# Later weight splits and scatters, scans two groups ahead and fixed input rings in a fused attention, expert and max-out kernel

## Chip, cores and metric

The kernel runs on one core of a Trainium2 chip. The metric is the device time of one execution in microseconds (us), the median of several runs. Rows of the trace come from one profiled execution.

## What is computed

Three layers in a row, all in float32 at the ends:

```python
for t in range(S):                      # B,H,S,D = 4,8,768,48
    state = alpha[t][:, None] * state + k[t] (x) v[t]
    y[t] = q[t] @ state                 # linear attention with decay
x = y as 3072 rows of 384
expert = argmax(xn @ en.T); gate = softmax(...)[expert]
x = gate * (relu(x @ w1[expert]) @ w2[expert])      # 8 experts, F = 1024
h = max(x @ w1, x @ w2, x @ w3); out = h @ w_out    # 384 -> 768 -> 384
```

## The kernel before

**Stage 1: groups.** The attention is done in 24 groups of 128 tokens (`NT`), all eight heads of a batch entry at once, six groups per batch entry. The code's loop `for g in range(NT)` writes out the order of instructions on every engine by hand (`manual_schedule`): each engine runs its own queue in exactly that order and waits on semaphores. For one group:

- `load(i)` brings the inputs of two groups (`at` decays, `kt`, `qt`, `vt`) through SP's queue, from tile pools with 3 or 4 buffers; a buffer is written again only when its last reader is done.
- `undo`, `invert`, `decay` (L270 to L293): two scans on VectorE (DVE), a reciprocal, then a product on GpSimd (POOL) that scales `qt`. They stand three groups ahead of the group that is finished.
- `spread` (L295): two copies on ScalarE (ACT) that put the scaled `qt` into the block tile `bdq`, two groups ahead.
- `keys`: a DVE product that scales `kt`.
- `scores` (TensorE, PE, L315), `causal` (DVE, L323), `sv` (PE, L350), `qs` (PE, L358, then the ACT copy `xt`, L361). In the first group of a batch entry `qs` has no products.
- `ranges` (ACT, L308): an absolute sum for a check at the end.
- `by_token` (PE, L368, then two ACT instructions), `kback` (PE transposes and an ACT copy), `logits` (DVE), `update` (PE, L389, then DVE products into `sbar`).

**Routing and scatters.** After 4 (later 2) groups a generator `route(i)` takes the argmax of their logits and counts places for the tokens: five DVE steps, then counting products on PE (`rk`, L418 to L421), then four DVE steps. `slot("P")`, `slot("A")` and so on step it on at marked places of the loop, by a string with a letter for each step. Its last step makes four (two) token groups `ready`, and `scatter` (L480, an indirect DMA issued by POOL) writes a group's 128 rows to `xs` in memory. The first scatter waits for the eight `zero_rows` DMAs (L238). When 18 groups have been scattered, `fetch_first` reads back the first 224 rows of expert 0 (`xa`).

**Weights.** `load_w` brings raw expert weights at the groups in `LOADS`. `split_w` cuts them into a high and a low part: two ACT casts (L222, L223) at the end of a group in `SPLITS`, and in the next group, after `slot("P")`, a POOL and a DVE subtraction (L225, L226).

**The end of stage 1.** `turn_first` transposes `xa`, the last `route` is run with the product `up` of the first weights beside it, the last scatters go out, and `fetch(0)` reads expert 0's further rows (`xb`), which waits for every scatter. **Stage 2** (from about 183 us) is the experts and the max-out layer, an almost gapless stream of PE products.

Of the kernel before, what the change touches and what calls it, by code (L numbers as in the profile page):

```python
# [35 lines left out]
CAP = max(CAPS)  # L36
AW = 224
AG = 18
NA = 5
LOADS = (8, 11, 16, 20)  # L40
SPLITS = (12, 14, 16, 18, 20)
ROW = DM + 2
TB = 512
BLOCKS = (256,) + (TB,) * 5 + (256,)
# [14 lines left out]
def fused_kernel(ctx, tc, qT, kT, aT, vn, emb, tau, w1, w2, m1, m2, m3, mo,  # L59
# [27 lines left out]
    loads = {}  # L87
    W = NP * C
    WE = NP * CE

    def load(i):

        b, c2 = divmod(i, NCH // 2)
        w = 2 * W
        o = c2 * w
        we = 2 * WE
        at = ld.tile([HR, we + 1], F32, tag="at", name=f"at_{i}", bufs=3)
        kt = ld.tile([HR, w], F32, tag="kt", name=f"kt_{i}")
        qt = ld.tile([HR, w], F32, tag="qt", name=f"qt_{i}")
        vt = ld.tile([128, 2, NP, HR], F32, tag="vt", name=f"vt_{i}")  # L100
        loads[i] = (at, kt, qt, vt)
        if i > 0:
            nc.sync.dma_start(at, aT[b, :, c2 * we:(c2 + 1) * we + 1])
            for t, src in ((kt, kT), (qt, qT)):
                nc.sync.dma_start(t, src[b, :, o:o + w])
            nc.sync.dma_start(vt, vn[b, :, 2 * c2:2 * c2 + 2])
            return
        for n in range(2):
            sl = slice(n * W, (n + 1) * W)
            if n == 0:  # L110
                nc.sync.dma_start(at[:, 0:WE + 1], aT[b, :, 0:WE + 1])
            nc.sync.dma_start(kt[:, sl], kT[b, :, sl])
            nc.sync.dma_start(qt[:, sl], qT[b, :, sl])
            if n == 0:
                nc.sync.dma_start(at[:, WE + 1:], aT[b, :, WE + 1:2 * WE + 1])
            nc.sync.dma_start(vt[:, n], vn[b, :, n])
# [70 lines left out]
        nc.gpsimd.iota(tokid[:, :, 1], pattern=[[1, NT]], base=0, channel_multiplier=NT)  # L187

    def constants_rest():
        nc.vector.tensor_sub(tri, mask, ident)  # L190
        nc.vector.tensor_copy(dec, dec_i)
        nc.vector.tensor_copy(base_b[0:1, :], base_i[0:1, :])

    def warm(ps, n):
        for _ in range(n):
# [74 lines left out]
    def undo(g):  # L270

        at, kt, qt, vt = loads[g // 2]
        o, oe = (g % 2) * W, (g % 2) * WE
        cur[g] = dict(bd=bdq[g % 3], qh=qt[:, o:o + W], kh=kt[:, o:o + W], v=vt[:, g % 2],
                      at=at[:, oe:oe + WE])
        cur[g]["PR"] = PR = wk.tile([HR, 2, WE], F32, tag="PR", name=f"PR_{g}", bufs=4)
        R = PR[:, 1]
        nc.vector.tensor_tensor_scan(R[:, ::-1], at[:, oe + 1:oe + WE + 1][:, ::-1], last[:, ::-1], 0.0, ALU.mult, ALU.add)
        cur[g]["R"] = R

    def by_pair(x, n=CE):
        return x.rearrange("p (a t) -> p a t", t=n)

    def invert(g):
        nc.vector.reciprocal(by_pair(first[g % 2])[:, :, 0], by_pair(cur[g]["R"])[:, :, 0])

    def decay(g):

        t = cur[g]
        P = t["PR"][:, 0]  # L290
        nc.vector.tensor_tensor_scan(P, t["at"], first[g % 2], 0.0, ALU.mult, ALU.add)  # L291
        qh = by_pair(t["qh"], C)
        nc.gpsimd.tensor_mul(qh, qh, by_pair(P)[:, :, 0:C])  # L293

    def spread(g):  # L295
        t = cur[g]
        for j in range(2):
            r = slice(j * 64, j * 64 + D)
            nc.scalar.copy(t["bd"][r, :, j], by_pair(t["qh"][r], C))
# [53 lines left out]
    def qs(g):  # L353
        t = cur[g]
        if g % NCH > 0:
            for p in range(NP):
                for j in range(2):
                    nc.tensor.matmul(t["xT"][own(j), p], t["sbar"][own(j), p], t["qh"][own(j), p * C:(p + 1) * C],  # L358
                                     start=False, stop=(p == NP - 1), skip_group_check=True)
        t["xs"] = wk.tile([HR, NP, C], F32, tag="xt", name=f"xt_{g}")  # L360
        nc.scalar.copy(t["xs"], t["xT"])  # L361
# [16 lines left out]
    def tokens(g):  # L378
        cur[g]["xr"] = xr = wk.tile([128, ROW], F32, tag="xr", name=f"xr_{g}", bufs=13)
        nc.gpsimd.tensor_copy(xr[:, DM:ROW].bitcast(I32), tokid[:, g])  # L380
# [95 lines left out]
    def step(it):  # L476
        return next(it, None)

    def scatter(pos, xr):
        r = nc.gpsimd.indirect_dma_start(out=xs, out_offset=bass.IndirectOffsetOnAxis(ap=pos, axis=0),  # L480
                                         in_=xr, in_offset=None, bounds_check=E * N - 1, oob_is_err=False).ins
        tc.declare_no_dep(r, group="scatters", reason="no two tokens take the same row")
        if 0 in exp:
            tc.declare_no_dep(r, group="first", reason="later tokens take other rows, or the general path runs")
        for z in zeroed:
            tc.add_manual_dep(r, z.name, DATA)
        tc.add_to_no_dep_group("scatters", r)
        placed.append(r)
# [122 lines left out]
    def slot(x):  # L611
        for c in chains:
            while c[1] and c[1][0] == x:
                step(c[0])
                c[1] = c[1][1:]

    with tc.manual_schedule():
        wm = ps_s.tile([128, 512], F32, tag="sr", name="wm")
        warm(wm, NWARM)
        emb_steps = embedding()  # L620
        step(emb_steps)
        for f in (undo, invert, decay, keys):
            f(0)
            step(emb_steps)
        spread(0)
        turn_base()
        undo(1)
        step(emb_steps)
        invert(1)
        step(emb_steps)  # L630
        decay(1)
        scores(0, 0)
        keys(1)
        scores(0, 1)
        for _ in emb_steps:
            pass
        embedding_turn()
        spread(1)
        causal(0, 0)
        causal(0, 1)  # L640
        wx = ps_x.tile([128, 512], F32, tag="xp", name="wx")
        warm(wx, NWARMX)
        load(2)
        constants_pool()
        kback(0)
        undo(2)
        invert(2)
        decay(2)
        ranges(0)
        constants_rest()  # L650
        zt = clear_scratch()

        ends = [sum(SIZES[:i + 1]) for i in range(len(SIZES))]
        splits = iter(())
        for g in range(NT):
            if g % 2 == 0 and 3 <= g // 2 + 3 < NT // 2:
                load(g // 2 + 3)
            if g < E:
                zero_rows(zt, g)
            if g in ends:  # L660
                i = ends.index(g)
                chains.append([route(i), "EEABCPABCE" if SIZES[i] > 2 else "EEEEEPABCE"])
            tokens(g)
            sv(g, 0)
            sv(g, 1)
            slot("P")
            step(splits)
            if g + 3 < NT:
                undo(g + 3)
            slot("A")  # L670
            for _ in range(1 if g < AG else 2):
                if g >= 8 and ready:
                    scatter(*ready.pop(0))
            if g > 0:
                by_token(g - 1)
            if g + 1 < NT:
                kback(g + 1)
            if g + 3 < NT:
                invert(g + 3)
            if g + 2 < NT:  # L680
                spread(g + 2)
            if g + 3 < NT:
                decay(g + 3)
            slot("B")
            if g + 1 < NT:
                for hf in range(2):
                    scores(g + 1, hf)
                    causal(g + 1, hf)
            slot("C")
            qs(g)  # L690
            if g + 1 < NT:
                ranges(g + 1)
            if g < NT - 2:
                keys(g + 2)
            if g > 0:
                logits(g - 1)
            update(g)
            slot("E")
            for _ in range(1 if g < AG else 2):
                if g >= 8 and ready:  # L700
                    scatter(*ready.pop(0))
            if len(placed) >= AG and 0 not in exp:
                fetch_first()
            if g in LOADS:
                load_w(LOADS.index(g))
            if g in SPLITS:
                splits = split_w(SPLITS.index(g))
                step(splits)
        turn_first()
        by_token(NT - 1)  # L710
        logits(NT - 1)
        chain = route(len(SIZES) - 1)
        for _ in range(5):
            step(chain)
        a = up(*order[0])
        for _ in chain:
            pass
        for r in ready:
            scatter(*r)
        a()  # L720
        keep(exp[0]["xa"], meta[0:AW], "ids_a")
        for n in (1, 2):
            up(*order[n])()
    pctx.close()
    ectx = ExitStack()
    pools["y"] = ectx.enter_context(tc.tile_pool(name="ps_y", bufs=1, space=PSUM))
# [426 lines left out]
```

## Time and profile before

| | us |
|---|---|
| median of 3 runs (709.54 to 712.46) | 711.03 |
| the profiled execution, its own time | 717.39 |
| span of its instructions | 715.7 |
| PE / DVE / ACT / POOL busy | 684.0 / 420.4 / 290.2 / 292.3 |

The span runs from the first to the last instruction; some 1.7 us of the execution's time lie around it. Busy shares are means over both stages. DVE is busy for 17 of the first 20 us and for less than a fifth of the last 100, so the means say nothing of stage 1. A matmul's end is modelled, so PE can look a little busier than it is.

### The profile page before, as it was taken

The numbers are of one execution on the slowest core, as the hardware profiler recorded it, in microseconds if no ns is written. First come the engines' busy times: TensorE is split into PE (matmuls) and PEld (weight loads), VectorE is DVE, ScalarE is ACT, GpSimd is POOL, SyncE is SP. The second block draws the span as 40 slices with busy tenths as digits, with TensorE's granted clock in tenths as the row PEclk, the third lists the DMA queues.
The fourth block names the chain that finished last, engine by engine and source line by source line (L and its number), as shares of the span: only waits on it lengthen the run. The fifth ranks groups of instructions, "written<-read, shape, count | busy, mean of one in ns | idle before, by whom it ended". The sixth has DMA issues, their size and how long they took to land. (4 is left out here: it accounts for less than half of the span.)

```text
span 715.7 us, 11937 instructions
## 1 busy us (share of the span) xinstructions
PE 684.0 (96%) x4467; PEld 610.0 (85%) x4467; DVE 420.4 (59%) x772; ACT 290.2 (41%) x617; POOL 292.3 (41%) x310
## 2 busy tenths in 40 slices
PE   7999799888999999999999999999999999999994
PEld 4788677668988999999999998888888898898994
DVE  8899698875478888888998699211311311303110
ACT  4676576654345445554545322321211212212221
POOL 5331746443134454554555366432333224233331
PEclk9999899999999999999999999999999999999998
DMA  9999965031355447546454220000000000000000
GB/s 231 265 274 247 255 185 187 23 108 69 109 153 174 136 147 212 173 157 204 139 178 149 46 67 24 24 15 30 1 22 23 1 22 23 0 23 23 12 34 26
DMA packets 30817, 75.01 MB, mean 105 GB/s; under 512 B 8600, under 2 KB 10400, under 8 KB 30752
## 3 DMA queue, kind: packets, MB, share of 16 engines
q1 hardware_dynamic: 26880, 64.68, 32.1%
q0 software_dynamic: 3840, 9.48, 3.7%
q8 instruction: 37, 0.61, 0.4%
q14 instruction: 28, 0.23, 0.1%
q10 hardware_dynamic: 32, 0.01, 0.0%
HBM read 62.26 MB, written 11.90 MB: 104 GB/s over the span
## 5 line engine op out<-in xcount | busy, mean ns | idle before, releaser
L931 DVE TENSOR_TENSOR t<-p,t 128x512 f32<-128x512 f32 (+1 forms) x84 | 51.6, 614 | 189.8 <-PE p L927 187.1
L925 PE MATMUL p<-bxh,m 128*128 128x512 f32 (+1 forms) x378 | 137.0, 362 | 0.0
L927 PE MATMUL p<-bxl,m 128*128 128x512 f32 (+1 forms) x378 | 137.0, 362 | 0.0
L926 PE MATMUL p<-bxh,m 128*128 128x512 f32 (+1 forms) x378 | 137.0, 362 | 0.0
L225 POOL TENSOR_TENSOR w<-r,w 128x384 fp32r<-128x384 f32 x64 | 71.4, 1117 | 80.8 <-ACT w L222 80.8
L938 POOL TENSOR_TENSOR fl<-t,fh 128x512 fp32r<-128x512 f32 (+1 forms) x36 | 43.5, 1208 | 139.3 <-ACT fh L937 104.2
L937 ACT CAST fh<-t 128x512 fp32r<-128x512 f32 (+1 forms) x42 | 23.5, 559 | 149.3 <-DVE t L931 149.3
L927 PEld LDWEIGHTS p<-bxl,m 128*128 128x128 f32 x378 | 71.1, 188 | 12.3
L925 PEld LDWEIGHTS p<-bxh,m 128*128 128x128 f32 x378 | 71.1, 188 | 11.9
L926 PEld LDWEIGHTS p<-bxh,m 128*128 128x128 f32 x378 | 71.1, 188 | 11.9
L572 PE MATMUL h<-xh,w 128*128 128x224 f32 (+8 forms) x207 | 72.2, 349 | 0.0
L573 PE MATMUL h<-xh,w 128*128 128x224 f32 (+8 forms) x207 | 70.4, 340 | 0.3 <-POOL w L225 0.3
L574 PE MATMUL h<-xl,w 128*128 128x224 f32 (+8 forms) x207 | 70.1, 339 | 0.0
L226 DVE TENSOR_TENSOR w<-r,w 128x384 fp32r<-128x384 f32 x64 | 60.4, 944 | 16.3 <-ACT w L223 16.3
L602 PE MATMUL y<-hl,w 128*128 128x464 f32 (+8 forms) x192 | 66.3, 345 | 0.0
L600 PE MATMUL y<-hh,w 128*128 128x464 f32 (+8 forms) x192 | 65.8, 343 | 0.0
L601 PE MATMUL y<-hh,w 128*128 128x464 f32 (+8 forms) x192 | 65.8, 343 | 0.0
L582 ACT ACTIVATE hh<-h 128x464 fp32r<-128x464 f32 (+8 forms) x64 | 32.0, 501 | 61.6 <-PE h L574 61.6
L315 PE MATMUL sc<-bdq,kt 112*128 112x256 f32 x192 | 51.1, 414 | 1.7 <-POOL bdq L175 1.7
L293 POOL TENSOR_TENSOR qt<-qt,PR 112x512 f32<-112x512 f32 x24 | 29.2, 1217 | 51.8 <-DVE PR L291 21.0
L583 DVE SCALAR_TENSOR_TENSOR hl<-h,hh 128x464 fp32r<-128x464 f32 (+8 forms) x64 | 36.2, 566 | 22.5 <-ACT hh L582 22.4
L946 PE MATMUL o<-wo,fh 128*128 128x384 f32 x144 | 48.4, 336 | 0.0
(206 smaller groups left out, 1415.4 us busy)
## 6 DMA issues: line engine op xcount, KB each, us to landing
r<-in_w SPq DMA_DIRECT2D x64, 384.0 KB, 3.7
cr_in_m<-in_m SPq DMA_DIRECT2D x18, 384.0 KB, 5.0
at<-in_aT SPq DMA_DIRECT2D x11, 451.9 KB, 11.4
kt<-in_kT SPq DMA_DIRECT2D x11, 448.0 KB, 11.6
qt<-in_qT SPq DMA_DIRECT2D x11, 448.0 KB, 10.0
vt<-in_vn SPq DMA_DIRECT2D x11, 448.0 KB, 11.1
exr<-xs_scratch SPq DMA_DIRECT2D x5, 675.5 KB, 6.1
xs_scratch<-zt SPq DMA_DIRECT2D x8, 289.5 KB, 12.6
```

The costliest lines, as they stand in the source:

```text
L225: nc.gpsimd.tensor_sub(a[:, 1], r1[:, k], a[:, 0].bitcast(F32))
L226: nc.vector.tensor_sub(b[:, 1], r2[:, k], b[:, 0].bitcast(F32))
L572: nc.tensor.matmul(hp, a[:, 0, k], t["xh"][:, k, c], start=(k == 0), stop=False)
L573: nc.tensor.matmul(hp, a[:, 1, k], t["xh"][:, k, c], start=False, stop=False)
L574: nc.tensor.matmul(hp, a[:, 0, k], t["xl"][:, k, c], start=False, stop=(k == KD - 1))
L600: nc.tensor.matmul(y, w[:, 0, sl], hh, start=(f == 0 and c.start == 0), stop=False, skip_group_check=True)
L601: nc.tensor.matmul(y, w[:, 1, sl], hh, start=False, stop=False, skip_group_check=True)
L602: nc.tensor.matmul(y, w[:, 0, sl], hl, start=False, stop=(f == NF1 - 1), skip_group_check=True)
L925: nc.tensor.matmul(pt, m[:, 0, k], xh[:, k], start=(k == 0), stop=False)
L926: nc.tensor.matmul(pt, m[:, 1, k], xh[:, k], start=False, stop=False)
L927: nc.tensor.matmul(pt, m[:, 0, k], xl[:, k], start=False, stop=(k == KD - 1))
L931: nc.vector.tensor_tensor(t0, pt, t0, op=ALU.max)
```

## The change

Seven things, all in stage 1:

1. `LOADS` go from (8, 11, 16, 20) to (14, 16, 21, 23), `SPLITS` from (12, 14, 16, 18, 20) to (19, 20, 21, 22, 23); the last split ends after the loop.
2. Scatters begin at group 9, not 8, and are at most two per group to the end (before: four per group from group 18). The first of a group's two stands behind the POOL product of `decay`, no longer ahead of it; `tokens` stands behind it too.
3. For pairs of groups the counting products move from the top of a group (`P`) to a new slot `Q` ahead of `qs` in the same group, and the four last steps follow in that group's `E`.
4. `undo`, `invert` and `decay` stand two groups ahead; `spread` stands one group ahead, at the top of the loop. The prologue loses one `undo`, `invert`, `decay` and `spread`.
5. `at`, `kt`, `qt` live in rings of four fixed tiles. From the fifth load on, each is read by two DMAs of 48 rows that leave out the 16 rows between two heads (before: one DMA of 112 rows). `at` gets one more buffer, `PR` one fewer.
6. Three small constants move from DVE to POOL and ACT; group 0's `qt` product moves from POOL to DVE.
7. After the loop two `up` products are issued before the last counting, not one.

```diff
-LOADS = (8, 11, 16, 20)
-SPLITS = (12, 14, 16, 18, 20)
+SC0 = 9
+LOADS = (14, 16, 21, 23)
+SPLITS = (19, 20, 21, 22, 23)
+NRING = 4
...
+    rings = {n: [ld.tile([HR, w], F32, tag=f"{n}{s}", name=f"{n}{s}", bufs=1) for s in range(NRING)]
+             for n, w in (("at", 2 * WE + 1), ("kt", 2 * W), ("qt", 2 * W))}
...
+            for r in (slice(0, HR),) if i < NRING else (slice(0, D), slice(64, HR)):
+                nc.sync.dma_start(at[r], aT[b, r, c2 * we:(c2 + 1) * we + 1])
+                for t, src in ((kt, kT), (qt, qT)):
+                    nc.sync.dma_start(t[r], src[b, r, o:o + w])
...
-        nc.vector.tensor_sub(tri, mask, ident)
-        nc.vector.tensor_copy(dec, dec_i)
-        nc.vector.tensor_copy(base_b[0:1, :], base_i[0:1, :])
+        nc.gpsimd.tensor_sub(tri, mask, ident)
+        nc.scalar.copy(dec, dec_i)
+        nc.scalar.copy(base_b[0:1, :], base_i[0:1, :])
...
-                chains.append([route(i), "EEABCPABCE" if SIZES[i] > 2 else "EEEEEPABCE"])
-            tokens(g)
+                chains.append([route(i), "EEABCPABCE" if SIZES[i] > 2 else "EEEEEQEEEE"])
+            if g + 1 < NT:
+                spread(g + 1)
             sv(g, 0)
             sv(g, 1)
             slot("P")
             step(splits)
-            if g + 3 < NT:
-                undo(g + 3)
+            if g + 2 < NT:
+                undo(g + 2)
             slot("A")
-            for _ in range(1 if g < AG else 2):
-                if g >= 8 and ready:
-                    scatter(*ready.pop(0))
             if g > 0:
                 by_token(g - 1)
             if g + 1 < NT:
                 kback(g + 1)
-            if g + 3 < NT:
-                invert(g + 3)
             if g + 2 < NT:
-                spread(g + 2)
-            if g + 3 < NT:
-                decay(g + 3)
+                invert(g + 2)
+                decay(g + 2)
+            if g >= SC0 and ready:
+                scatter(*ready.pop(0))
+            tokens(g)
             slot("B")
...
             slot("C")
+            slot("Q")
             qs(g)
...
             slot("E")
-            for _ in range(1 if g < AG else 2):
-                if g >= 8 and ready:
-                    scatter(*ready.pop(0))
+            if g >= SC0 and ready:
+                scatter(*ready.pop(0))
...
-        a = up(*order[0])
+        a = [up(*order[n]) for n in range(2)]
...
-        a()
+        for f in a:
+            f()
+        step(splits)
```

## Rows read from the trace of the kernel before

**Rows 1.** Windows: stretch, us, busy (count) PE PEld DVE ACT POOL, clock, DMA, GB/s.
```profile
26.78:59.41 32.63, 32.45 (x382) 27.54 (x384) 31.01 (x61) 25.03 (x53) 8.25 (x12) 1.00 1.04 269
26.78:142.19 115.41, 105.42 (x1144) 88.14 (x1144) 100.46 (x197) 78.27 (x167) 46.84 (x53) 0.94 0.75 203
65.10:83.20 18.10, 14.26 (x142) 11.75 (x144) 12.11 (x28) 8.17 (x17) 8.89 (x9) 0.81 1.04 256
112.56:121.61 9.05, 7.38 (x68) 5.80 (x70) 8.20 (x13) 3.81 (x9) 7.18 (x7) 0.81 0.80 256
142.19:169.43 27.24, 23.08 (x265) 19.20 (x266) 18.16 (x50) 14.60 (x32) 10.78 (x13) 0.94 0.25 86
148.93:159.58 10.65, 7.83 (x76) 6.46 (x78) 6.76 (x18) 5.05 (x11) 3.46 (x5) 0.84 0.39 132
183.00:715.70 532.70, 522.79 (x2818) 477.56 (x2818) 271.08 (x448) 179.45 (x378) 217.18 (x205) 1.00 0.26 78
```

**Rows 2.** Timeline of one undisturbed group: start, us, engine, line, tiles, idle before.
```profile
43.46 0.59 ACT L361 COPY xt<-xT 112x512 f32<-112x512 f32 x1 [0.68 <-PE xT L358]
...
44.07 1.06 ACT L308 ACTIVATE jk<-PR 112x1032 bf16<-112x1032 f32 x1
...
45.04 0.19 ACT L308 ACTIVATION_READ_ACCUMULATOR jk<-PR 112x1 f32 x1
...
46.19 1.91 PE L315 MATMUL sc<-bdq,kt 112*128 112x256 f32 x8
...
47.26 1.25 ACT L299 COPY bdq<-qt 48x512 f32<-48x512 f32 x2
...
48.00 1.18 POOL L293 TENSOR_TENSOR qt<-qt,PR 112x512 f32<-112x512 f32 x1 [4.01 <-DVE sm L413]
...
48.02 1.08 PE L358 MATMUL xT<-qt,sbar 48*48 48x128 f32 x16
...
49.15 0.58 ACT L361 COPY xt<-xT 112x512 f32<-112x512 f32 x1 [0.63 <-PE xT L358]
```

**Rows 3.** Timeline of POOL: the first scatter.
```profile
71.89 1.26 POOL L480 DMA_INDIRECT xs_scratch<-xr,pos  x1 [11.93 <-DMA r<-in_w]
```

**Rows 4.** Instructions of tile zt: the zeroing DMAs, their issues and landings.
```profile
L238 SPq DMA_DIRECT2D xs_scratch<-zt x8: 577/580/730, 21.8 to 51.8; - x8
...
DMA to landing us min/median/max: 9.9/12.6/13.2
```

**Rows 5.** Instructions of line 480: the scatters, their durations (ns) and landings.
```profile
L480 POOL DMA_INDIRECT xs_scratch<-xr,pos x24: 966/1000/1749, 71.9 to 176.5; - x24
...
DMA to landing us min/median/max: 2.6/3.4/9.6
```

**Rows 6.** Timeline of group 10: a POOL product beside a DVE product.
```profile
88.38 1.20 POOL L293 TENSOR_TENSOR qt<-qt,PR 112x512 f32<-112x512 f32 x1
88.48 1.66 DVE L304 TENSOR_TENSOR kt<-kt,PR 112x512 f32<-112x512 f32 x1
```

**Rows 7.** Timeline: a weight split in group 13, counting products in group 21.
```profile
96.13 0.51 ACT L223 CAST w<-r 128x384 fp32r<-128x384 f32 x1
...
96.67 1.05 DVE L226 TENSOR_TENSOR w<-r,w 128x384 fp32r<-128x384 f32 x1 [1.04 <-ACT w L223]
...
153.57 0.17 PE L420 MATMUL rk<-oh,ones_b 128*128 128x8 bf16 x1 [2.82 <-DVE oh L415]
```

**Rows 8.** Timeline of DVE at the start: the last scan before group 1's mask.
```profile
17.12 1.87 DVE L291 TENSOR_TENSOR_SCAN PR<-at,first 112x516 f32<-112x516 f32 x1
...
18.92 0.66 DVE L323 TENSOR_TENSOR ss<-sc,mask 128x512 f32<-128x512 f32 x1
```

**Rows 9.** Timeline of the end: last places, last scatter.
```profile
174.16 0.17 DVE L431 CAST pos<-sm 128x2 uint32<-128x2 f32 x1
...
176.47 0.98 POOL L480 DMA_INDIRECT xs_scratch<-xr,pos  x1 [0.30 <-issue]
```

**Rows 10.** DMA issues from 140 to 184 us: KB each, us to landing.
```profile
xa<-xs_scratch SPq DMA_DIRECT2D x1, 337.8 KB, 3.2
```

More of the change, by code (lines that the diff above doesn't have):

```diff
@@ L96, in load @@
         we = 2 * WE
-        at = ld.tile([HR, we + 1], F32, tag="at", name=f"at_{i}", bufs=3)
-        kt = ld.tile([HR, w], F32, tag="kt", name=f"kt_{i}")
-        qt = ld.tile([HR, w], F32, tag="qt", name=f"qt_{i}")
+        at, kt, qt = (rings[n][i % NRING] for n in ("at", "kt", "qt"))
         vt = ld.tile([128, 2, NP, HR], F32, tag="vt", name=f"vt_{i}")
@@ L102, in load @@
         if i > 0:
-            nc.sync.dma_start(at, aT[b, :, c2 * we:(c2 + 1) * we + 1])
-            for t, src in ((kt, kT), (qt, qT)):
-                nc.sync.dma_start(t, src[b, :, o:o + w])
+            for r in (slice(0, HR),) if i < NRING else (slice(0, D), slice(64, HR)):
+                nc.sync.dma_start(at[r], aT[b, r, c2 * we:(c2 + 1) * we + 1])
+                for t, src in ((kt, kT), (qt, qT)):
+                    nc.sync.dma_start(t[r], src[b, r, o:o + w])
             nc.sync.dma_start(vt, vn[b, :, 2 * c2:2 * c2 + 2])
@@ L275, in undo @@
                       at=at[:, oe:oe + WE])
-        cur[g]["PR"] = PR = wk.tile([HR, 2, WE], F32, tag="PR", name=f"PR_{g}", bufs=4)
+        cur[g]["PR"] = PR = wk.tile([HR, 2, WE], F32, tag="PR", name=f"PR_{g}", bufs=3)
         R = PR[:, 1]
@@ L292, in decay @@
         qh = by_pair(t["qh"], C)
-        nc.gpsimd.tensor_mul(qh, qh, by_pair(P)[:, :, 0:C])
+        (nc.gpsimd if g else nc.vector).tensor_mul(qh, qh, by_pair(P)[:, :, 0:C])
     def spread(g):
@@ L637, in fused_kernel @@
         embedding_turn()
-        spread(1)
         causal(0, 0)
@@ L645, in fused_kernel @@
         kback(0)
-        undo(2)
-        invert(2)
-        decay(2)
         ranges(0)
@@ L719, in fused_kernel @@
             scatter(*r)
-        a()
+        for f in a:
+            f()
+        step(splits)
         keep(exp[0]["xa"], meta[0:AW], "ids_a")
-        for n in (1, 2):
-            up(*order[n])()
+        up(*order[2])()
     pctx.close()
```

## The prediction

> **What bounds the kernel now.** I read the windows first, with edges at the `xt` copies that end a group's products. From 183.00 us on PE is busy 522.79 of 532.70 us at full clock [rows 1]; the change issues nothing there. So it is worth what it does to the time at which that stream starts, and I read stage 1 by groups.
>
> An undisturbed run of six groups (1 to 7) takes 32.63 us, with PE busy 32.45 and DVE 31.01 of it at full clock [rows 1]: both are full, PE a little more. A group takes 5.44 us there in the mean, and 5.69 where `qs` has products [rows 2]. DMA is full too (1.04), but nothing in that window waits for it. At that pace groups 1 to 19 would take 3 x 32.63 = 97.9 us; they take 115.41, and the granted clock falls to 0.94 [rows 1]. So 17.5 us are lost in the middle, in places that the windows show: groups 8 to 10 take 18.10 for 10.9, group 16 takes 9.05 and group 21 10.65 for 5.44, each with clock 0.81 to 0.84. There PE waited, then fell from 2.4 to 1.2 GHz for a while.
>
> The timelines give the causes. POOL sat idle 11.93 us ahead of its first scatter [rows 3], and the `qt` product of group 11 stood behind it. A weight split costs the full DVE queue 1.04 us of waiting for ACT's casts and 1.05 us of work [rows 7]; three of the five splits lie in groups 13, 15 and 17. PE stood 2.82 us in group 21 ahead of a counting product whose one-hot DVE had not reached [rows 7]. And where a scatter pushes POOL's `qt` product late, it falls on DVE's `kt` product, which then takes 1.66 us [rows 6].
>
> **The change part by part.** I make the sum against the profiled execution, 717.39 us, and carry its difference over to the median of 711.03.
>
> *Start.* Ahead of group 1's mask DVE no longer runs group 3's two scans. The last took 1.80 us from its start to the mask [rows 8]; both together at most twice that. But group 1's `spread` moves behind an ACT copy and `ranges` (1.06 + 0.19 [rows 2]), so `scores` comes later. I take -1.8; bounds 0 and -3.6. The constants and group 0's product move to engines that idle there; without that cover they cost some tenths, inside these bounds.
>
> *The nearer look-ahead costs something in each group.* In the new order ACT runs `xt`, `ranges`, and only then the next `spread`, for which the very next `scores` waits; before, `spread` had a whole group in hand. In the steady group `xt` starts at 43.46 and `ranges` ends at 45.23; with 1.25 for the two copies `bdq` is ready at 46.48, where PE was ready for `scores` at 46.19 [rows 2]. So PE waits 0.29 us, and the ring `xt`, `ranges`, `spread`, `scores`, `qs`, `xt` makes a group of 5.98 instead of 5.69. DVE's wait on that ring is late next, but its own 5.17 us a group (31.01 / 6) leaves it room. Six groups: 32.63 + 6 x 0.29 = 34.4; three times that is 103.1 for groups 1 to 19. The bounds are 0 (if an order of semaphores lets ACT start earlier) and 0.6 a group, twice the reading.
>
> *Splits out of the middle; counting at `Q`; scatters behind the `qt` product.* These remove what stood above 97.9 us. The splits' 2.1 us leave groups 13, 15 and 17. With the `qt` product ahead of the scatter it starts when `decay` ends, beside `causal`, as in the steady group (48.00 [rows 2]), and not beside `kt`. Behind a waiting scatter there is then only `tokens`, the second scatter and the next group's `qt`: 1.00 + 1.00 + 1.18 = 3.2 us [rows 2, 5], which fit in a group.
>
> *The first scatter.* The last zeroing DMA was issued at 51.8 and landed 12.6 us later by the median [rows 4], at 64.4; the scatter started at 71.89 [rows 3]. That leaves 7.5 us (6.9 to 10.2 by the slowest and fastest landing) that no releaser explains. In the new order the first scatter stands about a group later, so the zero rows are there, but those 7.5 us may be its own. The next `qt` product would then end 7.5 + 3.2 us after the last, where 5.98 for the group and 1.74 from its end to the next `spread` (49.18 to 49.15 + 1.77 [rows 2]) are covered: PE waits 3.0 us. Bounds 0 and 5.7. I take 3.0, since the only row of a first scatter is this one, and a low stretch of clock behind it: 0.84 over 10.65 us [rows 1] is 3.4 us at half clock, 1.7 us lost. The Trainium skill (GPSIMD Engine Reference, 2.1 Instruction dispatch) says that the first call of freshly loaded code on GpSimd pays about 6 us with no instruction to show for it. The trace's 6.9 or more is no less than that; with 6 in place of 7.5 the sum would be 1.5 us lower.
>
> So groups 1 to 19 take 103.1 + 3.0 + 1.7 = 107.8 for 115.41: -7.6.
>
> *Groups 20 to 23 take up the splits.* ACT's two casts (0.51 each [rows 7]) now stand between `ranges` and `spread`, in the ring: 5.98 + 1.02 = 7.0. Where scans remain (20, 21) DVE needs 5.17 + 1.05 + 1.04 = 7.26, which is more. Group 23 has no `scores` (1.83 from 46.19 to 48.02 [rows 2]): 4.15. That is 2 x 7.26 + 7.0 + 4.15 = 25.7, and with one low stretch (1.7) 27.4, for 27.24 [rows 1]: +0.2. The wait at the counting product goes, the splits come. Bounds -2 and +4.5.
>
> *End.* After the last places (174.16) before sent two scatters, the second at 176.47 and 1.28 us apart (0.98 + 0.30); `xb` follows when they have landed, and PE starts on it at 183.00 [rows 1, 9]. After has three there, one of group 23's two left over, so +1.3; and the last split's casts (1.02) stand ahead of `turn_first`'s copies on ACT, of which I put half on the path. The second `up` shortens PE's wait for the last one-hot, but `xb` ends last, so it gains nothing. +1.8, bounds +1.3 and +2.3. `fetch_first` comes two groups later: its chain behind the 19th scatter (1.00, 3.4 to land, 3.2 for `xa` [rows 5, 10]) is 7.6 us, under 7.0 + 4.15 of groups 22 and 23 by 3.5, less the wait for that scatter's places; I cost it at nothing, and at up to 2 us if that cover fails.
>
> *Rings and half loads.* Seven DMAs a load instead of four, a seventh fewer bytes in three of them. No wait of stage 1 after the start is for an input, so I count nothing; what hides it is that loads run groups ahead. Fewer bytes and later weights make the queues emptier when the first scatter goes out, which can only help its 7.5 us.
>
> Sum: -1.8 - 7.6 + 0.2 + 1.8 = -7.4, so 710.0 for the profiled execution and **703.6 us** for the median.
>
> **Rivals.** *A, more is won:* the 7.5 us ahead of the first scatter were traffic in full DMA queues and vanish, and no low stretch of clock remains: -7.4 - 3.0 - 1.7 - 1.7 = -13.8, 697 us. For it: DMA stood at 1.04 there [rows 1]. Against it: such a full queue let everything else through in 13.2 us at most [rows 4], and the scatter was not waiting for data.
>
> *B, the late groups take it back:* a pair's route adds nine DVE steps of 0.17 [rows 9] to each two groups, and they don't fit between split and scans. Then groups 20 to 22 each take 1.4 more (+4.3), and two more low stretches follow (+3.4): 711.3, no change. For it: group 21 was the slowest single group before [rows 1]. Against it: two of these groups lose their scans.
>
> *C, slower:* the 0.29 us at every `scores`, alone or with a late `bdq`, bring PE's clock down again and again. A low stretch costs 1.7 us; with one in every other of some 20 groups, eight beyond the two in the sum, +13.6 makes 717. It decides against the change from 4.4 further stretches on. For it: in the middle window the clock fell behind PE's waits [rows 1]. Against it: it stayed at 1.00 through a window in which PE sat idle 0.18 us in all, and the falls shown here follow waits of several times 0.29. The Trainium skill (TensorE: Matmul & The Clock Gate, HAM oscillation) describes kernels in which a wait at each tile lowers the clock at each tile, which is this rival; no row here shows it for waits so short.
>
> **How the numbers follow.** The forecast's own terms (698 to 708) get 0.53, A 0.15, B 0.18, C 0.14. A measurement of this kernel can tell 0.5%, 3.6 us, from no change: faster means below 707.5. The forecast and A lie there, 0.68; B is the same, 0.18; C is slower, 0.14. The range 695.5 to 711.5 takes in A and most of B and leaves out C.
>
> **What would show it.** Right: `xt` of group 1 near 25 us, then 5.9 to 6.1 us a group with `scores` released by the ACT copy into `bdq`; no DVE `kt` product near 1.66 us beside a `qt` product; no PE wait at counting products in groups 20 to 23; `xt` of group 19 near 133 and of group 23 near 160; PE's first transpose of `xb` near 176. A first scatter that starts without idle POOL time means A. The forecast is wrong if groups 2 to 6 take over 6.3 us, if the clock in groups 1 to 19 is below 0.94, or if group 20 to 23 take over 30 us.

## The result and the profile after

| | before | after |
|---|---|---|
| median of 15 runs, us | 710.77 | 704.45 |
| the profiled execution, its own time | 717.39 | 703.05 |
| span of its instructions | 715.7 | 701.4 |

The ratio after to before is 0.991, with a 95% interval of 0.989 to 0.9929: the change makes the kernel 0.9% faster. Two disturbed executions of the changed kernel, of 1053.58 and 1113.6 us, are in the 15 but not in the ratio.

The profiled executions differ by 14.3 us and the medians by 6.3, because the profiled execution of before stood 6.6 above the median of 710.77 and that of after 1.4 below its own. A later execution of the kernel before (below, `e12_before_again`) took 710.23 us. With it beside the first, the stretches between the `xt` copies read as follows. "Groups 1 to 19" runs from the `xt` copy of group 1 to that of group 19; a single group runs from the `xt` copy before it to its own.

| stretch, us | forecast against 717.39 | before, 717.39 | before again, 710.23 | after, 703.05 |
|---|---|---|---|---|
| to `xt` of group 1 | -1.8 | 26.78 | 27.20 | 23.30 |
| groups 1 to 19 | -7.6 | 115.41 | 105.98 | 103.14 |
| groups 19 to 23 | +0.2 | 27.24 | 28.90 | 26.14 |
| `xt` of group 23 to PE on `xb` | +1.8 | 13.57 | 13.42 | 15.41 |
| PE on `xb` to the end | 0 | 532.70 | 532.90 | 533.41 |

Windows of the changed kernel, in the columns of [rows 1]:

```profile
23.30:57.69 34.39, 33.55 (x383) 27.77 (x383) 31.36 (x61) 25.00 (x53) 8.22 (x13) 1.00 1.04 253
23.30:126.44 103.14, 100.77 (x1148) 83.71 (x1148) 95.14 (x194) 75.02 (x159) 41.41 (x49) 1.00 0.83 209
126.44:152.58 26.14, 22.91 (x265) 19.27 (x266) 22.27 (x51) 18.23 (x41) 15.87 (x19) 0.93 0.24 84
140.04:149.27 9.23, 7.45 (x81) 6.32 (x82) 6.70 (x17) 4.76 (x10) 5.82 (x7) 0.82 0.12 45
167.99:701.40 533.41, 523.03 (x2818) 477.51 (x2818) 271.57 (x448) 179.44 (x378) 216.78 (x205) 0.99 0.26 78
```

The first answers to the six groups of [rows 1]: 34.39 us for 32.63. The second has no low stretch of clock left (1.00 for 0.94). The lost time is now in the late groups: group 22, the fourth row, takes 9.23 us at 0.82.

Timeline of a steady group of the changed kernel, in the form of [rows 2]:

```profile
35.09 0.59 ACT L364 COPY xt<-xT 112x512 f32<-112x512 f32 x1 [1.60 <-PE xT L361]
35.57 1.07 ACT L311 ACTIVATE jk<-PR 112x1032 bf16<-112x1032 f32 x1
...
36.63 1.25 ACT L302 COPY bdq<-qt 48x512 f32<-48x512 f32 x2
...
37.93 1.99 PE L318 MATMUL sc<-bdq,kt 112*128 112x256 f32 x8 [0.36 <-ACT bdq L302]
...
40.97 0.58 ACT L364 COPY xt<-xT 112x512 f32<-112x512 f32 x1 [1.99 <-PE xT L361]
```

This is the ring of the prediction: `xt`, `ranges` (`jk`), `spread` (`bdq`), `scores`. PE waits 0.36 us for `bdq`, and the group takes 5.88 us.

POOL's timeline in the changed kernel, where [rows 3] had the first scatter:

```profile
68.05 1.18 POOL L296 TENSOR_TENSOR qt<-qt,PR 112x512 f32<-112x512 f32 x1 [4.78 <-DVE sm L416]
71.09 1.83 POOL L483 DMA_INDIRECT xs_scratch<-xr,pos  x1 [1.85 <-ACT xt L364]
```

POOL's idle time ahead of the first scatter fell from 11.93 us to 1.85. In the kernel before, the last of the scatter's waits had passed at 63.93, and the 8.0 us from there to its start are the 7.5 that the prediction could put down to nothing. Whether the change took them away was the main question.

### The profile page after: what moved, and what is told of

It reads as the page before. It is cut to its first block, busy times and chain, and to the rows that moved or that the text cites. A ratio compares the mean times of both kernels' runs of the same rounds, so it can differ in the third digit from the quotient of the medians.

```text
span 701.4 us, 11986 instructions
## 1 busy us (share of the span) xinstructions
PE 679.0 (97%) x4467; PEld 604.5 (86%) x4467; DVE 417.2 (59%) x770; ACT 290.4 (41%) x619; POOL 289.9 (41%) x310
## 5 line engine op out<-in xcount | busy, mean ns | idle before, releaser
L929 DVE TENSOR_TENSOR t<-p,t 128x512 f32<-128x512 f32 (+1 forms) x84 | 51.6, 614 | 189.8 <-PE p L925 187.1
L228 POOL TENSOR_TENSOR w<-r,w 128x384 fp32r<-128x384 f32 x64 | 71.5, 1119 | 77.3 <-ACT w L225 75.2
L229 DVE TENSOR_TENSOR w<-r,w 128x384 fp32r<-128x384 f32 x64 | 60.7, 949 | 13.7 <-ACT w L226 13.6
L296 POOL TENSOR_TENSOR qt<-qt,PR 112x512 f32<-112x512 f32 x23 | 27.5, 1195 | 71.2 <-DVE PR L294 35.4
L318 PE MATMUL sc<-bdq,kt 112*128 112x256 f32 x192 | 47.3, 389 | 4.0 <-ACT bdq L302 3.6
```

The lines of the kernel that those rows point to most:

```text
L228: nc.gpsimd.tensor_sub(a[:, 1], r1[:, k], a[:, 0].bitcast(F32))
L229: nc.vector.tensor_sub(b[:, 1], r2[:, k], b[:, 0].bitcast(F32))
L929: nc.vector.tensor_tensor(t0, pt, t0, op=ALU.max)
```

## The experiments

Ratios are to the kernel before, timed beside the edited one, with 95% intervals. An edit stands against the changed kernel unless it says otherwise. An engine's sequencer is the part that reads the engine's queue, waits on semaphores and hands instructions on; "the pause" is the time in which POOL's sequencer stands ahead of the first scatter though the semaphores it waits for have come.

**Late weights alone** (kernel before):

```diff
-LOADS = (8, 11, 16, 20)
-SPLITS = (12, 14, 16, 18, 20)
+LOADS = (14, 16, 21, 23)
+SPLITS = (19, 20, 21, 22, 23)
...
+        step(splits)
```

> The kernel before, with only the weight loads and splits moved to the later groups. Theory 'splits': three splits of 2.1 us of DVE time leave groups 13, 15 and 17 and the low clock behind them goes, the late groups take most of it back: 1 to 4 us less than before (ratio 0.994 to 0.999), and POOL still stands some 7 us or more idle ahead of its first scatter, beyond the landing of the zero rows. Rival 'weight traffic': that idle time came from the weight loads in the DMA queues; with them gone it falls under 3 us and the ratio is 0.990 or lower. Rival 'order': the gain is in the order of scans and scatters, and this part alone gives 1.000.

0.9959 (0.9929 to 0.9988), as the splits' theory had it: this part alone brings some 2.9 of the 6.3 us. Groups 1 to 19 took 103.69 us, 19 to 23 27.77. The pause was still 6.35 us (61.28 to 67.63), with the DMA engines still full (100.7%), so the weight loads did not cause it.

**Early weights** (the reverse edit, in the changed kernel):

> The changed kernel with the weight loads and splits back at the groups of before. Theory 'splits': groups 13, 15, 17 take about 2 us more each and groups 19 to 23 some 3 us less, so +2 to +4 us over the changed kernel (ratio to before 0.994 to 0.997). Rival 'weight traffic': POOL's wait ahead of its first scatter comes back (over 5 us) and the ratio is near 1.000. Rival 'order': nothing is lost, 0.991 or a little less, because the late groups are free of splits.

0.9949 (0.9926 to 0.9972). With a split in them again, groups 15 and 17 took 6.74 and 6.72 us for 5.91 and 5.88, and group 13 6.74 for 6.51; groups 19 to 23, with fewer splits, took 25.22 for 26.14. So a group with a split lost 0.2 to 0.8 us, not the 2 expected; with what follows in groups 14, 16 and 18, groups 13 to 19 took 2.9 more (43.80 for 40.94). But group 11 took 10.51 for 5.91, behind a pause of 6.88 us at the first scatter. The median stands where the splits' theory put it; this profile could have been read for the traffic of weights, and a later run showed that it must not be (`e5_after_again`).

**Scatters early:**

```diff
-SC0 = 9
+SC0 = 8
...
             slot("A")
+            if g >= SC0 and ready:
+                scatter(*ready.pop(0))
...
-            if g >= SC0 and ready:
-                scatter(*ready.pop(0))
             tokens(g)
```

> The changed kernel with the first scatter of a group back ahead of the products of by_token and of the POOL product of decay, and scatters from group 8 on. Theory 'place': the first scatter stands in POOL's queue until the zero rows have landed, about 3 us after it is its turn, with group 10's qt product behind it, and goes as soon as they are there; PE loses 0 to 3 us there and little in later groups: ratio 0.990 to 0.995. Rival 'first call': some 7 us pass between the landing of the zero rows and the scatter's start, as before, and with the low clock behind it the ratio is 0.997 or more.

0.9943 (0.9917 to 0.997). The first scatter started at 63.73, 0.9 us after the last of its waits had passed (62.84). Groups 1 to 19 took 104.19. So the first indirect DMA has no fixed price of several microseconds. No pause of over 1 us stands on POOL there.

**`ranges` behind `spread`:**

```diff
             if g + 1 < NT:
                 spread(g + 1)
+            if g > 0:
+                ranges(g)
...
-            if g + 1 < NT:
-                ranges(g + 1)
```

> The changed kernel with the ACT instruction of ranges moved behind the next group's two spread copies. Theory 'ring': a group takes 5.89 us because xt, ranges, spread and scores follow each other; with 1.07 us out of that ring a group takes 5.4 to 5.7 us, and groups 1 to 19 some 3 to 5 us less than 103.1: ratio 0.985 to 0.988. Rival 'DVE and PE full': a group stays at 5.8 to 5.9 because the next bound is as near, ratio 0.990 to 0.992.

0.9906 (0.9864 to 0.9948). Steady groups took 5.66 to 5.72 where the changed kernel has 5.88 to 5.91: the ring is confirmed. The gain was gone by group 11, which took 11.44 us behind a pause of 6.0 us at the first scatter.

**The changed kernel again:**

> The changed kernel once more, unchanged. POOL's dispatch pauses behind its first scatter's waits for 2.3 us in the profiled execution of it, for 6.0 and 6.9 us in two variants whose POOL queue is the same up to there. Theory 'fetch': the pause is the fetch of POOL's next instructions through the DMA queues and differs from execution to execution, 2 to 8 us, so this look can show either; ratio 0.989 to 0.993. Rival 'place': the two longer pauses came from what those variants changed, and this look shows 2 to 3 us again.

0.9904 (0.9875 to 0.9933). The profiled execution took 707.73 us, and a long pause was there in the same kernel. POOL's timeline; the scatter line's sequencer instructions (the second `MOVE` is the one that came late, at 75.7); then the DMA view of the time in which the sequencer stood (68.4 to 75.7): share of the 16 engines in 40 slices, and by queue and kind the packets, MB and share.

```profile
67.91 1.18 POOL L296 TENSOR_TENSOR qt<-qt,PR 112x512 f32<-112x512 f32 x1 [4.78 <-DVE sm L416]
75.86 1.14 POOL L483 DMA_INDIRECT xs_scratch<-xr,pos  x1 [6.77 <-ACT xt L364]
```

```profile
L483 POOLq EVENT_SEMAPHORE  x3: 17/17/43, 68.3 to 75.7; - x3
L483 POOLq MOVE  x2: 29/29/29, 68.3 to 75.7; - x2
```

```profile
DMA  9494999979959999989999999996999999979979
...
q1 hardware_dynamic: 439, 1.37, 100.3%
q14 instruction: 1, 0.01, 0.6%
```

The same view of the first profiled execution of the changed kernel, 68.5 to 70.9 us:

```profile
DMA  0004000000400000000000000000000094990254
...
q1 hardware_dynamic: 26, 0.09, 19.3%
q14 instruction: 1, 0.01, 1.2%
```

In both, the scatter's waits have passed, the next instruction in POOL's queue (the `MOVE`) waits for no semaphore that the trace shows, and one packet of kind "instruction" (8 KB) lands in between. The sequencer goes on 1.3 to 1.8 us after that packet's end (69.57 and 70.89; 73.84 and 75.67). With the DMA engines mostly idle this took 2.31 us, with full ones 7.22. Group 11 then took 11.07 us instead of 5.91, and groups 1 to 19 108.29 instead of 103.14. In the profiled execution of before the same pause is 7.76 us (63.93 to 71.69, the packet ends at 70.00).

**POOL's instructions moved on by 50 places:**

```diff
         nc.gpsimd.memset(bdq[2], 0.0)
+        for _ in range(50):
+            nc.gpsimd.memset(pad, 0.0)
```

> The changed kernel with 50 memsets of one element in POOL's queue near the start, 4 to 6 us, where POOL has no other work; they only move all later POOL instructions 50 places on. Theory 'fetch': the pause belongs to a place in POOL's instruction stream, so it moves ahead to the start (at most some us of idle POOL time before 13 us) and the first scatter starts without it; groups 10 and 11 keep 5.9 us; ratio 0.986 to 0.991, and the highest times come down. Rival 'first call': the pause belongs to the first indirect DMA and stays there, 2 us or more, with the ratio at 0.991.

0.9917 (0.9885 to 0.9949). POOL's timeline at the first scatter, and the DMA view of 67.9 to 68.7 us, which has no instruction packet:

```profile
67.84 1.17 POOL L299 TENSOR_TENSOR qt<-qt,PR 112x512 f32<-112x512 f32 x1 [4.78 <-DVE sm L419]
69.20 1.49 POOL L486 DMA_INDIRECT xs_scratch<-xr,pos  x1 [0.18 <-DMA qt<-in_qT]
```

```profile
q1 hardware_dynamic: 52, 0.16, 101.7%
```

The scatter follows the product by 0.18 us, with the DMA engines full, and groups 10 and 11 took 5.89 and 5.91. The pause therefore belongs to a place in POOL's instruction stream, not to the scatter and not to its data. The 8 KB packet near 69 us is gone, and one now lands at 14.9 to 15.6, where POOL is idle.

The median is no lower: the expected 0.986 to 0.991 was missed by a little. Groups 19 to 23 took 27.66 for 26.14 in the profiled execution, since the low stretch of clock in group 22 was longer there than in the changed kernel (9.23 us at 0.82):

```profile
140.27:150.71 10.44, 8.65 (x68) 7.13 (x70) 6.72 (x17) 4.76 (x11) 5.82 (x7) 0.67 0.21 72
```

The next run has such a group 22 too, without the memsets, so they are not shown to lengthen it. The times lie closer, 703.12 to 705.33, where the unchanged kernel beside it had 701.70 to 709.48; but these are 6 runs against 11, and the 5 of the next run, which has a pause, lie closer still. So that the memsets narrow the times is not shown.

**Whole rows:**

```diff
-            for r in (slice(0, HR),) if i < NRING else (slice(0, D), slice(64, HR)):
+            for r in (slice(0, HR),):
```

> The changed kernel with all loads of at, kt and qt as one DMA of 112 rows, as before, in the fixed rings. Theory 'nothing waits for inputs': 0.990 to 0.993, the same as the changed kernel; DMA queues stay full some us longer. Rival 'traffic': fuller queues make the pause ahead of the first scatter 6 us or more and the ratio 0.995 or more.

0.9904 (0.9871 to 0.9938); groups 1 to 19 in 102.82 us, the pause 2.3 us (share of the DMA engines 51.6%). Groups 19 to 23 took 28.03 in the profiled execution, with group 22 at 10.79 us and clock 0.68. The ratio is that of the changed kernel beside it (0.9904): the half loads cost and bring nothing that can be measured.

**`ranges` behind `spread`, and the 50 memsets:**

> The changed kernel with ranges behind the spread copies and the 50 memsets. Theory 'ring and fetch': groups of 5.66 us as in the run with ranges moved alone, and no stretch of low clock behind the first scatter: groups 1 to 19 in 98 to 100 us, ratio 0.983 to 0.987. Rival 'first call': the stretch near 73 us stays and the ratio is 0.990.

0.9859 (0.9825 to 0.9892), median 700.29. Its windows:

```profile
23.15:55.78 32.63, 32.45 (x383) 27.54 (x383) 30.95 (x61) 24.52 (x53) 8.69 (x13) 1.00 1.05 241
23.15:121.60 98.45, 97.95 (x1148) 83.03 (x1148) 93.74 (x194) 73.74 (x159) 41.33 (x49) 1.00 0.89 222
121.60:148.75 27.15, 23.05 (x265) 19.23 (x266) 23.05 (x55) 18.22 (x40) 15.97 (x19) 0.94 0.27 96
```

The six groups take 32.63 us again, as in [rows 1], and groups 1 to 19 98.45 where the prediction had put the undisturbed pace at 97.9. The late groups gained nothing: 27.15 us for 26.14.

**The 50 memsets in the kernel before:**

> The kernel before with 50 one-element memsets near the start of POOL's queue and nothing else. Theory 'fetch': the 7.8 us between the landing of the zero rows and the first scatter vanish, the scatter starts within 1 us of its last wait, groups 9 and 10 take 3 to 7 us less than 18.1 and the ratio is 0.990 to 0.996. Rival 'queue': the pause belongs to full DMA queues in any case, wherever POOL's instructions stand; it stays, and the ratio is 0.998 to 1.002.

1.0001 (0.9979 to 1.0022): the ratio was missed, and stands where the rival `queue` had put it, but the pause is gone, as that rival had excluded. The first scatter started at 63.27, 0.17 us after `tokens`; groups 9 to 11 took 16.82 us at full clock, where [rows 1] has 18.10 for 9 and 10 alone:

```profile
68.23:85.05 16.82, 16.82 (x208) 14.29 (x210) 16.30 (x37) 12.30 (x26) 10.34 (x11) 1.00 0.90 282
```

But the memsets took 7.28 us of POOL at 9.41, and group 1's `qt` product stood behind them (16.69 for 10.96): `xt` of group 0 came at 22.45 for 19.19, that of group 1 at 29.91 for 26.78 (27.20 in the second execution of before). That cost of the experiment itself, some 3 us, hides what is gained. The ratio comes out at 1 if the pause costs about as much in an average execution of before, which nothing measures.

**The POOL half of a split behind `tokens`:**

```diff
         yield
-        nc.gpsimd.tensor_sub(a[:, 1], r1[:, k], a[:, 0].bitcast(F32))
         nc.vector.tensor_sub(b[:, 1], r2[:, k], b[:, 0].bitcast(F32))
+        yield
+        nc.gpsimd.tensor_sub(a[:, 1], r1[:, k], a[:, 0].bitcast(F32))
...
             tokens(g)
+            step(splits)
...
+        step(splits)
```

> The changed kernel with only the POOL half of a weight split moved behind tokens, so that it no longer stands beside DVE's half and the scan behind it. Theory 'POOL and DVE in each other's way': the scan of 2.58 us goes back to 1.2, DVE's half of 2.11 to some 1.2, PE no longer waits 1.78 us in group 22, and groups 19 to 23 take 2 to 4 us less than 26.1: ratio 0.985 to 0.988. Rival 'DVE is full there anyway': groups 20 to 22 stay at 6.6 to 6.9 us and the ratio at 0.990.

0.991 (0.9875 to 0.9946), groups 19 to 23 in 26.46 us: the theory fell. In the changed kernel POOL's half (L228), behind a scatter (L483), stands beside a scan and beside DVE's half (L229), and PE waits in group 22:

```profile
128.95 0.98 POOL L483 DMA_INDIRECT xs_scratch<-xr,pos  x1 [0.16 <-POOL xr L383]
129.49 2.58 DVE L281 TENSOR_TENSOR_SCAN PR<-at,last 112x516 f32<-112x516 f32 x1
129.95 1.02 POOL L228 TENSOR_TENSOR w<-r,w 128x384 fp32r<-128x384 f32 x1
...
137.00 2.11 DVE L229 TENSOR_TENSOR w<-r,w 128x384 fp32r<-128x384 f32 x1
137.66 1.03 POOL L228 TENSOR_TENSOR w<-r,w 128x384 fp32r<-128x384 f32 x1
...
142.37 0.87 PE L353 MATMUL xT<-ss,vt 128*64 128x128 f32 x6 [1.78 <-DVE ss L326]
```

In the edited kernel DVE's half takes 0.56 us, but `update`'s product (0.36 in the changed kernel) now stands beside POOL's half, and in group 22 beside the end of a scatter as well, and takes 1.84 and 1.49, and in group 23 PE waits for the one-hot behind it:

```profile
141.88 1.27 POOL L484 DMA_INDIRECT xs_scratch<-xr,pos  x1 [0.16 <-POOL qt L297]
...
142.67 1.84 DVE L399 TENSOR_TENSOR sbar<-sbar,PR 112x192 f32<-112x192 f32 x1
...
143.28 1.01 POOL L230 TENSOR_TENSOR w<-r,w 128x384 fp32r<-128x384 f32 x1
...
149.09 1.49 DVE L399 TENSOR_TENSOR sbar<-sbar,PR 112x192 f32<-112x192 f32 x1
...
151.54 0.17 PE L424 MATMUL rk<-oh,ones_b 128*128 128x8 bf16 x1 [2.30 <-DVE oh L419]
```

The collision moved; it did not go. Group 22 took 6.70 us for 9.23, and group 23 6.26 for 3.31.

**All three edits:**

> The changed kernel with ranges behind the spread copies, the 50 memsets, and the POOL half of a split behind tokens. If the late groups lose 2 to 4 us as in the theory of the run with the POOL half alone, the ratio is 0.980 to 0.983, against 0.986 without that part; if DVE is full there anyway, 0.985 to 0.987.

0.985 (0.9812 to 0.9888), median 699.48: with the run without the POOL half it is the fastest version, and the two cannot be told apart.

**The kernel before again:**

> The kernel before, unchanged, in one more profiled execution. Its profiled execution of 717.39 us stands 6.4 above its median. Theory 'fetch': the pause ahead of the first scatter differs from execution to execution; in one of 708 to 712 us groups 9 and 10 take 11 to 15 us, not 18.1, and from PE's first product of the later rows on nothing differs. Rival: the difference lies elsewhere, in the start or in stage 2, and groups 9 and 10 take 17 to 19 us again.

710.23 us, one execution. The pause was 4.08 us (60.82 to 64.90), and groups 9 and 10 took 11.44 us, not 18.10. Another 3.3 us lie in groups 16, 18 and 19 (9.05, 7.29 and 7.61 us in the first execution, 7.38, 6.51 and 6.72 in this); no run was made for them. Groups 19 to 23 are 1.7 us slower here, and from there on nothing differs by more than 0.2.

## Why the prediction was right, point by point

The forecast of 703.6 lies 0.9 from the median. That is in part luck. The sum was made against the execution of 717.39 us, and against that one it missed by 6.9 (-7.4 for -14.3): `xt` of group 23 and PE on `xb` came at 152.58 and 167.99, not near 160 and 176. Carried over to the median it fits, and it agrees with the -7.2 between 710.23 and 703.05, but not term by term. Against 710.23 the stretches of the table give -3.9, -2.8, -2.8, +2.0 and +0.5 for the forecast -1.8, -7.6, +0.2, +1.8 and 0: groups 1 to 19 gave 4.8 less than forecast, the start 2.1 and the late groups 3.0 more.

*The ring: right.* Six groups were to take 34.4 us and took 34.39, groups 1 to 19 without a stall 103.1 and took 103.14; a steady group took 5.88 to 5.91 for 5.98, with PE's wait at 0.36 for 0.29. Taking `ranges` out of the ring gave 32.63 and 98.45.

*The first scatter: the cause was wrong, and the price came in one execution of two.* The prediction took the 7.5 us for the scatter's own and charged 3.0 + 1.7 = 4.7. One execution lost nothing (pause 2.31), another 5.15 (103.14 to 108.29, pause 7.22). The step that failed is "those 7.5 us may be its own": they are POOL's wait for its next instructions, which happens to fall at the first scatter in both kernels, and its length goes with the DMA queues of that execution. In the nine profiled executions that have it, it was 2.3 to 2.5 us in the three in which the share of the DMA engines was 19 to 52% during it, and 4.1 to 7.8 in the six in which it was 100 to 104%; the four with the memsets have none. Rival A had the mechanism (traffic in full queues) and its time for the profiled execution (-13.8 for -14.3), but most of that is the long execution of before: the change does not take the pause away, and a low stretch of clock remains in group 22. It can make a pause dearer, because the `qt` product is needed sooner. A pause of 6.35 us cost groups 9 to 11 2.1 us in the old order (18.88 with late weights for 16.82 with the memsets); 6.0 us cost group 11 5.7 in the new one (11.44 for 5.72 in the two runs with `ranges` moved). But when it ends counts as much as how long it is: in the first execution of before, where the pause began 2.7 us later than with late weights (63.93 for 61.28) and lasted 7.76, groups 9 to 11 lost 7.0 us in the old order too (23.79 for 16.82).

The Trainium skill (Runtime: NRT & Kernel Launch, Instruction fetch mechanics) says that an engine's sequencer fetches its instructions in blocks through a DMA queue of its own, and that crossing a block is mostly hidden. The packets of kind "instruction" agree with the blocks; the trace has two queues of them and does not say which engine a packet is for, so that the one at the pause is POOL's rests on the run with the memsets. The pauses of 2.3 to 7.8 us on POOL do not agree with "mostly hidden". The rule of the Trainium skill that the prediction cited (GPSIMD Engine Reference, 2.1 Instruction dispatch: some 6 us at the first call of freshly loaded code) is not what these runs show: where the pause is absent, the first scatter followed its waits by 0.9 us (scatters early) or POOL's last work by 0.18 (the memsets). That code was freshly loaded here no run shows.

*Start: the mechanism was right, the term mis-sized.* -1.8 was forecast with a bound of -3.6; measured were -3.5 and -3.9. PE's row of the kernel before, the wait for the mask of [rows 8], and two rows of the changed kernel, the second of which answers to it:

```profile
19.63 1.25 PE L350 MATMUL xT<-ss,vt 128*64 128x128 f32 x16 [2.49 <-DVE ss L323]
```

```profile
15.55 1.99 PE L318 MATMUL sc<-bdq,kt 112*128 112x256 f32 x8 [1.46 <-ACT bdq L302]
...
17.88 0.30 PE L353 MATMUL xT<-ss,vt 128*48 128x128 f32 x1
```

Before, PE began on the product that needs the mask at 19.63, now at 17.88. So group 1's products start 1.75 us earlier, the -1.8 of the forecast. The other 1.7 us are clock, which the term left out. From there to `xt` of group 1, before and after:

```profile
19.63:26.78 7.15, 7.15 (x56) 5.93 (x58) 5.71 (x9) 3.81 (x10) 2.53 (x4) 0.76 1.05 257
```

```profile
17.88:23.30 5.42, 5.42 (x66) 4.58 (x63) 5.35 (x9) 2.46 (x6) 1.46 (x2) 1.00 1.05 270
```

PE is busy throughout in both, at a granted clock of 0.76 behind the wait of 2.49 us, and of 1.00 behind that of 1.46.

*Groups 13, 15 and 17: right in kind, too dear.* Late weights alone gave 0.9959; putting them back took the changed kernel to 0.9949. The cost of 2.1 us a split was read in the order of before. There it shows a group later, as cut at `xt`: groups 14, 16 and 18 took 7.38, 7.38 and 6.51 us in the second execution of before, and 5.83, 5.41 and 4.98 with late weights. In the new order they made groups 13 to 19 2.9 us longer.

*Late groups: right in kind, 1.3 too dear.* +0.2 was forecast; -1.1 came out (-2.8 against the second execution of before). Groups 20 and 21 took 6.70 and 6.90 for the 7.26 forecast, group 22 9.23 for 8.7 (7.0 and the one low stretch expected, 1.7), group 23 3.31 for 4.15. Rival B's wait, a pair's steps between split and scans, is there as PE's 1.78 us in group 22, but DVE's half of the split, at 2.11 us, is the longest step ahead of it. The wait at the counting product of [rows 7] is gone.

*End: the size was right, its making was not.* 15.41 us for 13.57, +1.8. But no third scatter stands behind the last places, for which the forecast counted +1.3. The one left over went at 155.90, while POOL had nothing else to do, and two follow the last places, as before:

```profile
155.90 0.98 POOL L483 DMA_INDIRECT xs_scratch<-xr,pos  x1 [0.30 <-issue]
158.34 0.17 DVE L434 CAST pos<-sm 128x2 uint32<-128x2 f32 x1
159.38 1.03 POOL L483 DMA_INDIRECT xs_scratch<-xr,pos  x1 [2.50 <-ACT hs L585]
160.72 0.98 POOL L483 DMA_INDIRECT xs_scratch<-xr,pos  x1 [0.30 <-issue]
```

Instead the last places come 1.0 us later behind `xt` of group 23 (5.76 us for 4.73), and ACT's two casts, 1.02 us, stand ahead of them: `by_token`'s copy of group 23 starts 2.82 us behind that `xt` for 1.82. The forecast had put half of the casts on the path.

```profile
153.33 0.51 ACT L225 CAST w<-r 128x384 fp32r<-128x384 f32 x1 [0.16 <-DMA r<-in_w]
154.27 0.51 ACT L226 CAST w<-r 128x384 fp32r<-128x384 f32 x1 [0.43 <-DMA r<-in_w]
154.69 0.83 ACT L451 CAST xh<-ta 128x224 fp32r<-128x224 f32 x3
155.40 0.50 ACT L374 COPY xr<-xp 128x384 f32<-128x384 f32 x1
```

The rest lies behind the last scatter (160.72, 8.14 us behind `xt` of group 23; before 7.04): PE starts on `xb` 7.27 us after it for 6.53. `xb` takes 4.35 us from its issue to PE's first product (163.64 to 167.99), before 3.19 (179.81 to 183.00). Why it takes longer no run shows.

```profile
167.99 0.70 PE L519 MATMUL t<-ident,xb 112*128 112x112 f32 x5 [2.04 <-DMA xb<-xs_scratch]
```

*Rival C did not come.* The clock stayed at 1.00 through 103 us in which PE waited at `scores` by up to 0.4 us. *Half loads: right*, nothing (0.9904 without them); the fixed rings were not run alone.

What stays open: how DVE's and POOL's work of the late groups can be laid out so that none collides, why the low stretch of clock in group 22 takes it to 9.2 to 9.4 us in some runs and 10.4 to 10.8 in others, and why the median of the changed kernel with the memsets is not below that without them.

## What to carry to other kernels

Before a stall is charged to the instruction that it precedes, read the same kernel in a second profiled execution, and what the engine's sequencer and the instruction packets do: here a wait for instructions looked like the price of a first scatter. A few cheap instructions put ahead of it tell the two apart. What such a pause costs depends on how soon the work behind it is needed, so a nearer look-ahead buys its time with less cover. A sum that fits a median can still hold terms that are off by several microseconds each way; hold it against each stretch. And an instruction off the critical path, like `ranges`, costs its time where it stands in a ring: moving it behind the one that is waited for gave 4.7 us over 18 groups (103.14 to 98.45, no long pause in either), where the whole change had won 6.3.

## What the runs showed of the hardware that was not expected

- GpSimd waits for its own instructions, which come in 8 KB packets through the same DMA engines as the data: 2.3 to 2.5 us with the engines partly idle (19 to 52%), 4.1 to 7.8 with full ones, always at the same place of its stream, and not at all once that stream was moved on by 50 places. On VectorE and ScalarE no idle stretch of over 1 us between 3 and 180 us ends at an instruction that waits for nothing, in any of the 14 profiled executions.
- A DVE product of 0.36 us takes up to 1.84, a scan of 1.2 us 2.58 and a subtraction of 0.56 us 2.11 beside a POOL subtraction of 1.02 and the scatter or copy just ahead of it. The Trainium skill (SBUF — State Buffer, SBUF: two separate sides) says that the two engines lock a port pair that they share for a whole instruction; the lengths agree in kind. Each is 1.1 to 1.6 us over the short time, which is more than the subtraction alone lasts; that the scatter or copy ahead of it holds DVE too is not shown.
